# Where tile 1's first half statistics stand on VectorE: behind tile 0's first normalised half instead of ahead of tile 0's reciprocal

## The chip, the cores and the metric

The kernel runs on one core of one Trainium2 chip. The metric is the device time of one execution in microseconds (us), lower is better. A profile shows one execution. The experiments ran on four different chips, so kernels are compared by ratios within the same rounds. The "span" of a profile or run is the core's own time from first to last instruction; it is about 1.7 us less than the time.

## The reference, cut to what matters

```python
xn = _layernorm(x, axis=-1)                      # x: 2048 rows of 512, bf16
return x + _A_ref(xn, ...) + _B_ref(xn, ...)     # A: a state-space scan, B: a gated FFN

def _layernorm(x, axis=-1, eps=1e-5):
    m = jnp.mean(x, axis=axis, keepdims=True)
    v = jnp.var(x, axis=axis, keepdims=True)
    return (x - m) / jnp.sqrt(v + eps)
```

Every matmul of A and B reads `xn`, so nothing useful can run on TensorE before the first rows are normalised and transposed. The rows come in 16 tiles of 128. The first four tiles are the head of the kernel, and the change lies there.

## The kernel before: the parts that count

The program is a list of tasks with dependencies. A static scheduler puts them into one instruction list per engine; `order=` pins a task behind another. The loads of the head, and who issues them (SP's queue unless `eng="act"`):

```python
x_load(0)
x_load(1)
act_q = [dma("ld_touch", ..., eng="act")]
act_q.append(wg_load("a0", 0, 2, eng="act", ...))   # gate weights, 448 KB
x_load(2)                                           # each x tile: 128 KB
act_q.append(wg_load("a1", 2, 3, eng="act", ...))   # 224 KB
wg_load("a2", 3, 4)                                 # 224 KB
x_load(3)
# ... cut: further weights, x tiles 4 to 7
```

VectorE's pinned order for the four tiles of the head:

```python
last = ln_stat0(0, (bn_full(0),))        # tile 0: statistics, aggregate; ScalarE then takes the square root
last = bn_half(1, 0, order=(last,))      # tile 1: statistics of its first 256 columns
for a in range(4):
    last = g.add("dve", lambda e, a=a: e.reciprocal(out=rstd[:, a:a + 1], in_=sd0[:, a:a + 1]), ..., order=(last,))
    last = ln_half(a, 0, order=(last,))  # normalise columns 0 to 255 of tile a
    if a < 3:
        last = bn_half(a + 1, 1, order=(last,))
        last = ln_stat0(a + 1, (last,))
    last = ln_half(a, 1, order=(last,))
    if a < 2:
        last = bn_half(a + 2, 0, order=(last,))
```

Tile 0 uses statistics of all its 512 columns at once, the others of two halves. Each normalised half goes through two PE transposes into one PSUM bank, and ScalarE (for tile 3 VectorE) copies it to `xnT`. PE's order in the head is fixed: transposes of tile 0 (two pairs, with a few warming matmuls between, whose results nobody uses), 14 gate matmuls on tile 0's first half, the **third pair of transposes** (tile 1, first half), 14 gate matmuls on tile 0's second half, and so on; then the first 512-wide matmuls.

## Time and profile before

| | before |
|---|---|
| time, median of the runs in hand at the prediction | 180.02 us (179.74 to 180.13) |
| profiled execution | 180.3 us, span 178.6 us |
| PE busy / VectorE busy | 97% / 91% of the span |
| PE's share of the chain that ended last | 95% |

The page's first part, engine by engine (PE is TensorE, PEld its weight loads, DVE VectorE, ACT ScalarE, POOL GpSimd; SP, further down, is SyncE, which issues most loads; L509 means line 509 of the kernel):

```profile
span 178.6 us, 2421 instructions
PE 173.3 (97%) x929; PEld 83.9 (47%) x937; DVE 162.3 (91%) x281; ACT 88.7 (50%) x114; POOL 9.9 (6%) x21
```

The chain of waits that ended last, in order of time (start, duration, what):

```profile
1.25 3.50 DMA x_sb<-in_A_x_dram
...
4.78 0.43 DVE st L509
...
6.63 0.27 PE pb L565 x2
6.91 0.78 PE pb L780 x14
7.69 0.11 PE pb L565 x2
...
14.14 11.22 PE pb L739 x52
```

From 6.63 us on the chain is PE, piece against piece, to the end. What can be won is won ahead of that. There, the chain goes through a load of x (`x_sb`), then the half statistics at 4.78. The VectorE timeline of before shows what they held up (start, duration, instruction; in brackets the idle time before it and what ended it):

```profile
4.78 0.43 DVE L509 BATCH_NORM_STATS2 st<-x_sb 128x6 f32<-128x256 bf16 x1 [0.77 <-DMA x_sb<-in_A_x_dram]
5.12 0.15 DVE L531 RECIPROCAL rstd<-sd 128x1 f32<-128x1 f32 x1
5.31 0.35 DVE L514 TENSOR_SCALAR xn_sb<-x_sb,mv,rstd 128x256 bf16<-128x256 bf16 x1
...
6.36 0.42 DVE L509 BATCH_NORM_STATS2 st<-x_sb 128x6 f32<-128x256 bf16 x1
6.71 0.16 DVE L531 RECIPROCAL rstd<-sd 128x1 f32<-128x1 f32 x1
```

L509 at 4.78 is tile 1's half statistics, waiting 0.77 us for tile 1's data. Tile 0's reciprocal (L531) stands behind it, though its operand, ScalarE's square root, was ready at 4.33. L509 at 6.36 is tile 2's, in front of tile 1's reciprocal. And the PE timeline, with the first two pairs of transposes, the first gate group, and the third pair at 7.53:

```profile
5.80 0.27 PE L565 MATMUL pb<-ident,xn_sb 128*128 128x128 bf16 x2 [1.41 <-DVE xn_sb L514]
...
6.63 0.27 PE L565 MATMUL pb<-ident,xn_sb 128*128 128x128 bf16 x2 [0.23 <-ACT xnT L577]
6.75 0.94 PE L780 MATMUL pb<-xnT,wg 128*128 128x128 bf16 x14
7.53 0.28 PE L565 MATMUL pb<-ident,xn_sb 128*128 128x128 bf16 x2
```

The trace also records when each load's semaphore is complete. I call that the landing. In this execution tile 0 landed at 3.07 us, tile 1 at 4.76, tile 2 at 6.32.

### The profile page before, as it was taken

How to read it: one execution, taken by the hardware profiler on the slowest of the kernel's cores; microseconds unless marked ns; L12 is line 12 of the kernel's file. 1: busy time of each engine (PE TensorE's matmuls, PEld its weight loads, DVE VectorE, ACT ScalarE, POOL GpSimd, SP SyncE). 2: the span in 40 equal slices, each digit the busy share in tenths (PEclk: the TensorE clock that was granted, in tenths of full speed). 3: DMA queues.
4: the chain of work that ended last, by engine and by line, in shares of the span. 5: the costliest groups of instructions: out<-in, count | busy, mean ns of one | idle time of the engine just before them, and what ended most of it. 6: DMA issues, size and time to landing. Idle time of an engine off the chain costs nothing.

```text
span 178.6 us, 2421 instructions
## 1 busy us (share of the span) xinstructions
PE 173.3 (97%) x929; PEld 83.9 (47%) x937; DVE 162.3 (91%) x281; ACT 88.7 (50%) x114; POOL 9.9 (6%) x21
## 2 busy tenths in 40 slices
PE   7699999999999999999999999999999999999994
PEld 3595444443444444444444444444444444444743
DVE  1858985798899999999999999999999999999983
ACT  4369998999799957016565651000965620000000
POOL 3013400002300000040000000000000000000000
DMA  5995562669360000002420000001100000000122
GB/s 167 367 332 113 128 118 51 141 170 355 103 121 0 0 0 0 0 13 79 95 54 0 0 0 4 0 0 63 55 0 4 0 0 0 0 0 4 59 88 88
DMA packets 22978, 12.37 MB, mean 69 GB/s; under 512 B 15192, under 2 KB 22968, under 8 KB 22968
## 3 DMA queue, kind: packets, MB, share of 16 engines
q1 hardware_dynamic: 22472, 11.54, 23.5%
q10 hardware_dynamic: 496, 0.69, 1.2%
q8 instruction: 7, 0.11, 0.3%
q14 instruction: 3, 0.02, 0.1%
HBM read 6.46 MB, written 2.10 MB: 48 GB/s over the span
## 4 chain that ended last, share of the span: by engine, by line
PE 95%; DMA 2%; DVE 1%; issue 1%; SPq 0%; ACT 0%
PE pb L739 35%; PE pb L937 21%; PE pb L854 15%; PE pb L950 15%; PE pb L780 4%; DMA x_sb<-in_A_x_dram 2%; PE pb L817 2%; PE pb L827 1%; PE pb L565 1%; DVE st L509 0%; SPq L400 0%; ACT xnT L577 0%; DVE xn_sb L514 0%; DVE x_sb L955 0%; PE pb L562 0%
## 5 line engine op out<-in xcount | busy, mean ns | idle before, releaser
L894 DVE TENSOR_TENSOR_SCAN rot<-sm,car,rot 128x512 bf16<-128x512 f32 x32 | 39.0, 1267 | 0.1
L937 PE MATMUL pb<-wd,hT 128*128 128x512 bf16 (+3 forms) x194 | 38.1, 355 | 0.2
L739 PE MATMUL pb<-xnT,wu 128*128 128x512 bf16 x160 | 37.3, 379 | 0.0
L739 PE MATMUL pb<-xnT,wg 128*128 128x512 bf16 x132 | 31.3, 379 | 0.0
L950 PE MATMUL pb<-W,hss 128*128 128x512 bf16 (+2 forms) x140 | 28.1, 355 | 0.2
L854 PE MATMUL pb<-xnT,BT 128*128 128x512 bf16 x128 | 28.1, 379 | 0.0
L937 PEld LDWEIGHTS pb<-wd,hT 128*128 128x128 bf16 (+1 forms) x198 | 18.5, 98 | 19.9
L739 PEld LDWEIGHTS pb<-xnT,wu 128*128 128x128 bf16 x160 | 15.6, 98 | 18.9 <-issue 0.2
L751 ACT ACTIVATE sg<-pb 128x1024 bf16<-128x1024 f32 x20 | 20.1, 1025 | 8.6 <-PE pb L739 7.5
L807 ACT ACTIVATE uf<-pb 128x1024 bf16<-128x1024 f32 x20 | 20.6, 1028 | 6.8 <-PE pb L739 5.9
L950 PEld LDWEIGHTS pb<-W,hss 128*128 128x128 bf16 x144 | 13.5, 98 | 14.3
L739 PEld LDWEIGHTS pb<-xnT,wg 128*128 128x128 bf16 x132 | 12.7, 98 | 15.7 <-issue 0.8
L854 PEld LDWEIGHTS pb<-xnT,BT 128*128 128x128 bf16 x128 | 12.5, 98 | 15.1
L861 ACT ACTIVATE u_sb<-pb 128x1024 bf16<-128x1024 f32 x16 | 16.4, 1026 | 4.5 <-PE pb L854 4.2
L809 DVE TENSOR_TENSOR hT<-sg,uf 128x1024 bf16<-128x1024 bf16 x20 | 13.5, 682 | 1.0 <-ACT uf L807 0.9
L885 DVE TENSOR_TENSOR rot<-u_sb,cosT 128x2048 bf16<-128x2048 bf16 x8 | 9.7, 1219 | 2.8 <-ACT cosT L700 2.8
L955 DVE TENSOR_TENSOR x_sb<-pb,x_sb 128x512 bf16<-128x512 f32 (+2 forms) x18 | 10.9, 624 | 1.5 <-PE pb L950 1.4
L836 ACT ACTIVATE sg<-pb 96x1024 bf16<-96x1024 f32 x2 | 2.0, 1019 | 17.3 <-PE pb L817 17.3
L503 ACT ACTIVATE xn_sb<-x_sb,nmr,rstd 128x512 bf16<-128x512 bf16 x8 | 5.9, 802 | 9.3 <-DVE nmr L500 9.3
L885 DVE TENSOR_TENSOR rot<-rot,cosT 128x2048 bf16<-128x2048 bf16 x8 | 9.7, 1218 | 0.1
L885 DVE TENSOR_TENSOR rot<-rot,sin 128x2048 bf16<-128x2048 bf16 x8 | 9.8, 1219 | 0.0
L885 DVE TENSOR_TENSOR rot<-u_sb,sin 128x2048 bf16<-128x2048 bf16 x8 | 9.7, 1217 | 0.0
(78 smaller groups left out, 142.5 us busy)
## 6 DMA issues: line engine op xcount, KB each, us to landing
out_dram<-x_sb SPq DMA_DIRECT2D x15, 128.0 KB, 1.7
x_sb<-in_A_x_dram SPq DMA_DIRECT2D x3, 512.0 KB, 7.5
wd<-in_B_w_down_dram SPq DMA_DIRECT2D x1, 1280.0 KB, 7.1
wu<-in_B_w_up_dram SPq DMA_DIRECT2D x1, 768.0 KB, 5.4
wu<-in_B_w_up_dram SPq DMA_DIRECT2D x1, 608.0 KB, 7.5
x_sb<-in_A_x_dram SPq DMA_DIRECT2D x4, 128.0 KB, 4.1
wg<-in_B_w_gate_dram SPq DMA_DIRECT2D x1, 480.0 KB, 6.4
wg<-in_B_w_gate_dram ACTq DMA_DIRECT2D x1, 448.0 KB, 4.5
```

The costliest lines, as they stand in the source:

```text
L739: inst = e.matmul(pbank[0:fs, bk, :].rearrange("p (j t) -> p j t", j=4), lhsT=w[:, kt, i * 128:i * 128 + fs], rhs=xnT[:, c % 2, :, kt, :], ...
L751: g.add("act", lambda e: e.activation(out=sg[rows, sl, 0:n, :].rearrange("p a t -> p (a t)"), in_=pair_f32(rows, bk, 512 * n), func=AF.Sil ...
L780: inst = e.matmul(pbank[:, bk, q * 128:(q + 1) * 128], lhsT=wg[:, kt, i * 128:(i + 1) * 128], rhs=xnT[:, 0, q, kt, :], start=(kt == 0), st ...
L807: g.add("act", lambda e: e.activation(out=uf[rows, ul, 0:n, :].rearrange("p a t -> p (a t)"), in_=pair_f32(rows, bk, 512 * n), func=AF.Ide ...
L809: g.add("dve", lambda e: e.tensor_tensor(out=hT[rows, hb, i0:i0 + n, :], in0=sg[rows, sl, 0:n, :], in1=uf[rows, ul, 0:n, :], op=ALU.mult), ...
L854: inst = e.matmul(pbank[:, bk, :].rearrange("p (j t) -> p j t", j=4), lhsT=BT[:, ri, kt, pt * 128:(pt + 1) * 128], rhs=xnT[:, c % 2, :, kt ...
L861: g.add("act", lambda e: e.activation(out=u_sb[:, us].rearrange("p r t -> p (r t)"), in_=pair_f32(slice(0, 128), b0), func=AF.Identity), r ...
L885: tt = lambda out, a, b, op, r, w, nm: g.add("dve", lambda e: e.tensor_tensor(out=out, in0=a, in1=b, op=op), reads=r, writes=w, name="%s_% ...
L894: g.add("dve", lambda e, A0=A0, A1=A1, k=k, ri=ri, pt=pt: e.tensor_tensor_scan(out=A1[:, k, ri, :], data0=rr[:, pt:pt + 1].to_broadcast([1 ...
L937: inst = e.matmul(pbank[:, bk, 0:nc_], lhsT=hT[0:fs, hb, i, lt * 128:(lt + 1) * 128], rhs=wd[0:fs, i, c0:c0 + nc_], start=(i == 0), stop=F ...
L950: inst = e.matmul(pbank[:, bk, 0:nc_], lhsT=hss[:, hb, pt, ri, lt * 128:(lt + 1) * 128], rhs=W12[:, ri, pt, c0:c0 + nc_], start=False, sto ...
L955: g.add("dve", lambda e, bk=bk, a=a, c0=c0, nc_=nc_: e.tensor_tensor(out=x_sb[:, a, c0:c0 + nc_], in0=pbank[:, bk, 0:nc_], in1=x_sb[:, a, ...
```

## The change

The intent: tile 0 should not wait for tile 1's data. Its reciprocal and first normalised half go ahead, and tile 1's first half statistics come behind them.

```diff
             last = ln_stat0(0, (bn_full(0),))
-            last = bn_half(1, 0, order=(last,))
             for a in range(4):
                 last = g.add("dve", ... e.reciprocal(...) ..., order=(last,))
                 last = ln_half(a, 0, order=(last,))
+                if a == 0:
+                    last = bn_half(1, 0, order=(last,))
+                    last = ln_half(0, 1, order=(last,))
                 if a < 3:
                     last = bn_half(a + 1, 1, order=(last,))
                     last = ln_stat0(a + 1, (last,))
-                last = ln_half(a, 1, order=(last,))
+                if a:
+                    last = ln_half(a, 1, order=(last,))
                 if a < 2:
                     last = bn_half(a + 2, 0, order=(last,))
```

No instruction is added or removed.

## The prediction

> **What bounds the kernel.** TensorE. The page gives it 97% of the 178.6 us span, and the chain of waits that ended last is 95% PE. From 6.63 us on, that chain has hardly anything but PE groups, one against the next. Only the head is something else: the load of x tile 1, VectorE, ScalarE. A change in the head is worth what it moves the start of the unbroken PE stretch, and no more.
>
> **What the change moves.** No instruction is added or removed; VectorE's order in the head changes. In the VectorE timeline, the statistics of tile 0 end at 4.01 us and ScalarE's square root of tile 0 at 4.33, but VectorE stands idle (0.77 us, released by the x DMA) until 4.78, because the half statistics of tile 1 are next and x tile 1 has landed only at 4.76. The Trainium skill ("DVE: scalar operands, raw-bit mode, write accounting and state across instructions") calls the DVE's queue "one in-order queue"; this trace agrees: the reciprocal, ready at 4.33, runs at 5.12. After the change:
> - reciprocal 4.37 (was 5.12), first half of tile 0 4.57 to 4.92 (was 5.31), its PE transpose 5.06 (was 5.80), second transpose about 5.89 (was 6.63, after ScalarE's eviction), first gate matmuls about 6.01 (was 6.75). Their weights landed at 5.70.
> - Tile 1: second half of tile 0 at 5.17, second half statistics 5.38, aggregate 5.83 (was 6.02), square root done about 6.35 (was 6.67).
>
> **Why most of the 0.74 us is not kept.** The half statistics of tile 2 stand ahead of tile 1's reciprocal, and x tile 2's DMA is complete only at 6.33 us in this trace (before: that instruction started at 6.36, with no visible wait). The change brings VectorE there at 5.96; it waits until about 6.35. Then tile 1's reciprocal comes at about 6.70 (was 6.71), its first half at 6.90 to 7.25 (was 6.91). The transpose of tile 1 can start at 7.39, against 7.53 before, where it waited only for PE itself. So PE starts earlier, gets a new hole of about 0.4 us (6.95 to 7.39), and its unbroken stretch moves by about 0.14 us. Had x tile 2 landed early, the gain would be about 0.45 us (square root 6.35, reciprocal 6.39, transpose 7.08), and no more.
>
> After that the PE is unbroken as before.  Downstream waits have slack for 0.1 to 0.5 us: B's transposed load is complete at 22.8, needed at 25.4; the C weights are ready at 73.6, needed at 75.7; the last scan products at 168.5, needed at 171.1 (VectorE timeline against PE timeline). VectorE's work after 14.2 us is tied to the x4 load, not moved.
>
> **Prediction:** 179.83 us, between 179.45 and 180.15 with 80%. Faster by over 2%: 0.3%; same: 99.4%; slower: 0.3%.
>
> **What would show it.** VectorE timeline: no wait before the first reciprocal, which starts near 4.4; the x DMA's wait is now split: nothing or almost nothing before tile 1's first statistics (about 4.83), and a wait of about 0.2 us (engine-idle) before tile 2's. PE: first transpose near 5.06; first gate group near 6.0; a new wait for tile 1's normalised half (about 0.4 us) before the third pair of transposes; first 512-wide matmul at about 13.84 instead of 13.98.
>
> **What would make it wrong.** x tile 2 landing 0.2 us or more earlier in timed runs (gain up to 0.45), or later (gain to zero); the gate weights' loads (complete at 5.70, 6.61 and 7.17) becoming the wait; a later reorder on VectorE or ScalarE that costs the PE a wait; noise (0.4 us wide in three runs).

## The result, and the profile after

| | before | after |
|---|---|---|
| median of 4 timed runs | 179.96 us (179.74 to 180.13) | 179.99 us (179.85 to 180.09) |
| profiled execution: span | 178.6 us | 178.1 us |

The ratio of after to before is 1.0002, 95% interval 0.9984 to 1.0019. Ratios here are the mean time of one kernel's fast runs over that of the other's of the same rounds, so not quite the ratio of the medians quoted. So the time is the same, inside the predicted range. Yet the two profiles differ by 0.5 us in favour of after. The VectorE timeline of after:

```profile
4.34 0.16 DVE L530 RECIPROCAL rstd<-sd 128x1 f32<-128x1 f32 x1 [0.36 <-ACT sd L521]
4.54 0.35 DVE L514 TENSOR_SCALAR xn_sb<-x_sb,mv,rstd 128x256 bf16<-128x256 bf16 x1
4.80 0.42 DVE L509 BATCH_NORM_STATS2 st<-x_sb 128x6 f32<-128x256 bf16 x1
...
5.83 0.21 DVE L519 BATCH_NORM_AGGREGATE mv<-st 128x2 f32<-128x12 f32 x1
5.96 0.37 DVE L509 BATCH_NORM_STATS2 st<-x_sb 128x6 f32<-128x256 bf16 x1
6.41 0.16 DVE L530 RECIPROCAL rstd<-sd 128x1 f32<-128x1 f32 x1
```

The reciprocal of tile 0 now runs at 4.34, released by ScalarE, and tile 1's statistics at 4.80, with no wait. But tile 2's statistics at 5.96 did not wait either: in this execution tile 1 landed at 4.11 us and tile 2 at 5.40, far earlier than in the profile of before. No VectorE instruction can have done that; these loads wait for no engine, and were issued at 1.25 and 1.71 us in both profiles. The PE timeline and one line of the chain of after:

```profile
6.01 0.94 PE L783 MATMUL pb<-xnT,wg 128*128 128x128 bf16 x14
7.01 0.28 PE L568 MATMUL pb<-ident,xn_sb 128*128 128x128 bf16 x2
```

```profile
13.68 11.22 PE pb L742 x52
```

The third pair is at 7.01 instead of 7.53, and the 0.46 us by which the chain's 512-wide matmuls begin earlier (13.68 against 14.14) is kept to the end of the span. Two profiles therefore seem to show a gain of about half a microsecond which four timed runs do not show.

### The profile page after: what moved, and what is told of

It reads as the page before. It is cut to its first block, busy times and chain, and to the rows that moved or that the text cites. A ratio compares the mean times of both kernels' runs of the same rounds, so it can differ in the third digit from the quotient of the medians.

```text
span 178.1 us, 2421 instructions
## 1 busy us (share of the span) xinstructions
PE 174.4 (98%) x929; PEld 84.1 (47%) x937; DVE 162.3 (91%) x281; ACT 88.8 (50%) x114; POOL 10.3 (6%) x21
## 4 chain that ended last, share of the span: by engine, by line
PE 95%; DVE 2%; DMA 1%; issue 0%; ACT 0%
PE pb L742 36%; PE pb L940 21%; PE pb L857 16%; PE pb L953 15%; PE pb L783 3%; PE pb L820 2%; DMA x_sb<-in_A_x_dram 1%; PE pb L830 1%; PE pb L568 1%; DVE xn_sb L514 1%; DVE st L527 0%; DVE st L509 0%; ACT sd L521 0%; DVE mv L519 0%; DVE rstd L530 0%
## 5 line engine op out<-in xcount | busy, mean ns | idle before, releaser
L857 PE MATMUL pb<-xnT,BT 128*128 128x512 bf16 x128 | 28.1, 379 | 0.0
L857 PEld LDWEIGHTS pb<-xnT,BT 128*128 128x128 bf16 x128 | 12.5, 98 | 15.1
L503 ACT ACTIVATE xn_sb<-x_sb,nmr,rstd 128x512 bf16<-128x512 bf16 x8 | 5.9, 803 | 9.6 <-DVE nmr L500 9.6
```

What stands on the lines that cost most here:

```text
L503: g.add("act", lambda e, a=a: e.activation(out=xn_sb[:, a % NXN, :], in_=x_sb[:, a, :], func=AF.Identity, scale=rstd[:, a:a + 1], bias=nmr ...
L857: inst = e.matmul(pbank[:, bk, :].rearrange("p (j t) -> p j t", j=4), lhsT=BT[:, ri, kt, pt * 128:(pt + 1) * 128], rhs=xnT[:, c % 2, :, kt ...
```

## The experiments

Theory: **the two orders are decided by landings, which differ from one execution to the next.** If tile 1 lands late, the order of after is ahead; if it lands early, tile 1's half statistics fit under tile 0's square root in the order of before, and the order of after has put them into the path to tile 1's reciprocal for nothing. Rival: the head is really half a microsecond shorter, and it is **given back later**. Twelve kernels were run; all were correct. Ratios are to the kernel before in the same rounds.

| run | tile 1's load | tile 2's load | median us | ratio, 95% interval |
|---|---|---|---|---|
| e1_before_again | as is | as is | 179.79 | 1.0005 (0.9987 to 1.0022) |
| e1_after_again | as is | as is | 179.93 | 1.0008 (0.9994 to 1.0021) |
| e2_before_x1_late | third | second | 182.26 | 1.0136 (1.0112 to 1.0159) |
| e2_after_x1_late | third | second | 180.57 | 1.0051 (1.0034 to 1.0068) |
| e3_before_x_early | alone | behind weights | 182.31 | 1.0146 (1.0120 to 1.0172) |
| e3_after_x_early | alone | behind weights | 179.98 | 1.0025 (1.0004 to 1.0045) |
| e4_before_x1_late_warm | third | second | 181.50 | 1.0099 (1.0082 to 1.0116) |
| e5_before_x_first | alone | alone | 180.18 | 1.0007 (0.9994 to 1.0020) |
| e5_after_x_first | alone | alone | 180.43 | 1.0045 (1.0013 to 1.0076) |
| e6_before_x2_late | as is | last | 181.53 | 1.0077 (1.0057 to 1.0096) |
| e6_after_x2_late | as is | last | 181.06 | 1.0059 (1.0045 to 1.0074) |
| e7_before_x_first_x8_early | alone | alone | 179.83 | 1.0007 (0.9991 to 1.0023) |

### Both kernels once more, unchanged

No edit: these are second samples of the two heads.

> The kernel before, unchanged, as a second sample of its head. Landing theory (the sign and size of the change hang on when x tile 1 lands, and that differs between executions): time within 0.15 us of the kernel before; in its trace tile 1's x lands earlier than the 4.76 us of the first trace of before, about 4.1 to 4.5 us, and the third pair of transposes on PE starts at that landing plus 2.76 us (never before 6.76). Rival (the trace of before is typical and what the change gains at the head is given back later): x tile 1 lands at about 4.76 us again and that transpose starts at about 7.5 us.

> The kernel after, unchanged. Landing theory: ratio to before between 0.9990 and 1.0010; in its trace the third pair of transposes starts at 7.0 us if x tile 1 lands before 4.8 and x tile 2 before 6.0, at x tile 2's landing plus 1.0 us otherwise. Rival: the third pair starts about 0.45 us earlier than in the second trace of before, and a wait on PE that the kernel before does not have appears somewhere after 20 us.

The second profile of before has the span of after, 178.1 us. Its VectorE timeline:

```profile
4.34 0.43 DVE L509 BATCH_NORM_STATS2 st<-x_sb 128x6 f32<-128x256 bf16 x1 [0.36 <-DMA x_sb<-in_A_x_dram]
4.68 0.15 DVE L531 RECIPROCAL rstd<-sd 128x1 f32<-128x1 f32 x1
```

Tile 1 landed at 4.32 us here, not at 4.76, and the third pair of transposes ran at 7.09, which is that landing plus 2.77, as in the first profile (4.76 and 7.53):

```profile
7.09 0.28 PE L565 MATMUL pb<-ident,xn_sb 128*128 128x128 bf16 x2
```

The second profile of after shows tile 2 at 6.16 us and the wait that the prediction had spoken of, a short one:

```profile
5.88 0.21 DVE L519 BATCH_NORM_AGGREGATE mv<-st 128x2 f32<-128x12 f32 x1
6.18 0.43 DVE L509 BATCH_NORM_STATS2 st<-x_sb 128x6 f32<-128x256 bf16 x1
6.52 0.15 DVE L530 RECIPROCAL rstd<-sd 128x1 f32<-128x1 f32 x1
```

In the profile of after the statistics came 0.13 us behind the aggregate's start, here 0.30 us. The third pair came at 7.11, no earlier than in this second profile of before:

```profile
7.11 0.29 PE L568 MATMUL pb<-ident,xn_sb 128*128 128x128 bf16 x2 [0.21 <-DVE xn_sb L514]
```

PE is unbroken from there on in both. So the half microsecond between the first two profiles was mostly the landing of the loads: in this second pair the rival has no gain left that would have to be given back. (That an earlier head can be given back in other executions is shown further down, by e5.)

### Tile 1 made late

```diff
         x_load(0)
-        x_load(1)
+        x_load(2)
         act_q = [dma("ld_touch", ..., eng="act")]
         act_q.append(wg_load("a0", 0, 2, eng="act", ...))
-        x_load(2)
+        x_load(1)
```

> Kernel before with the loads of x tiles 1 and 2 swapped in their queue, so that tile 1 lands about 1.2 us later (5.4 to 6.3 us). Landing theory: the whole head follows tile 1's landing; third pair of transposes at landing plus 2.76 us, so 8.2 to 9.1 us; slower than before by 0.9 to 1.6 us. Rival (given back later): slower by less than 0.3 us, because a late head is absorbed downstream as the early one would be.

> Kernel after with the same swap. Landing theory: tile 0 goes ahead without tile 1 (first transpose at 5.05 us), third pair of transposes at tile 1's landing plus 2.23 us, so 7.6 to 8.6 us; faster than the swapped kernel before by 0.4 to 0.6 us. Rival (given back later): same as the swapped kernel before within 0.1 us.

The order of after is now 1.7 us faster (180.57 against 182.26). In the profile of after, tile 1 landed at 5.40 and the third pair came at 7.64, landing plus 2.24, as expected. In that of before, tile 1 landed at 5.86, but the third pair came at 9.34, not at 5.86 + 2.77 = 8.63. The time was 2.5 us over before, where at most 1.6 had been expected, and the distance between the two kernels three times the expected one: a second cost had been left out. The PE timeline of e2_before_x1_late shows it:

```profile
6.90 0.27 PE L565 MATMUL pb<-ident,xn_sb 128*128 128x128 bf16 x2 [2.09 <-DVE xn_sb L514]
...
7.85 1.70 PE L780 MATMUL pb<-xnT,wg 128*128 128x128 bf16 x14
...
9.55 1.70 PE L780 MATMUL pb<-xnT,wg 128*128 128x128 bf16 x14
...
11.26 0.95 PE L780 MATMUL pb<-xnT,wg 128*128 128x128 bf16 x14
```

Two groups of 14 took 1.70 us, the next one 0.95, and the granted clock (the share of TensorE's full rate, from the trace's clock records) was 1.00 from 6.0 to 7.8 us, 0.51 from 7.8 to 11.3, and 1.00 again after that. In the chain the same groups stand with 1.49 and 0.78 us, so 106 and 56 ns for each matmul. The Trainium skill ("TensorE: Matmul & The Clock Gate", section "Wait — 56ns, not 53.3ns?") gives 106.7 ns cold and 55.6 ns warm between starts of 128-column matmuls, and this trace agrees. PE had been idle for 2.09 us, waiting for tile 0, and then paid 0.71 us twice.

To test that, the swapped kernel before got 9 more warming matmuls ahead of the head (the scheduler's estimate was held, so the other engines' lists stayed the same):

```diff
-            pe_warm(9, 512, wbank)
+            pe_warm(18, 512, wbank)
```

> The kernel before with tile 1 landing late (loads of tiles 1 and 2 swapped), with 9 more warming matmuls at the start, so that PE has work until about 6.3 us. The swapped kernel before took 182.26 us, 1 us more than landing plus 2.76 us explains, and its trace shows the first two gate groups at 1.49 us instead of 0.78 each. Cold-array theory: with the extra warming both groups take about 0.78 us, and the time falls to about 180.8 us (180.5 to 181.3). Rival (the slow groups come of something else, as late gate weights): the groups stay at about 1.5 us and the time stays within 0.4 us of 182.26.

The groups took 0.78 us each again, as their first line in the PE timeline shows too:

```profile
8.33 0.94 PE L780 MATMUL pb<-xnT,wg 128*128 128x128 bf16 x14
```

The time fell by 0.76 us, to 181.50 (by the ratios, since the two ran in different rounds, by about 0.7). The fall is smaller than expected. In the profiled execution of this run tile 1 landed at 6.34, and the third pair came at 9.11, again landing plus 2.77. So the cold array accounts for part of what the late kernel lost, and the landing for at least part of the rest; the split in the timed runs isn't known, since only one execution of each has a profile. The granted clocks help a little: of the six runs of e2_before_x1_late, two (182.94, which is the profiled one, and 182.43) have 0.991, which is what 3.4 us at half rate make of 181 us, and the fastest (181.37) has 0.999. The other three read 1.0, which is also what an execution without clock records gets.

### Tile 1 made early

```diff
-        act_q.append(wg_load("a0", 0, 2, eng="act", ...))
+        wg_load("a0", 0, 2)
         x_load(2)
-        act_q.append(wg_load("a1", 2, 3, eng="act", ...))
+        wg_load("a1", 2, 3)
```

> Kernel before with the gate weights' loads moved from ScalarE's queue into the x loads' own queue, behind x tile 1, so that tile 1 lands without competition (about 3.5 us) and tile 2 at about 5.5. Landing theory: tile 1's half statistics fit under tile 0's square root, the reciprocal starts at about 4.36, the third pair of transposes at about 6.76 us (7.09 in the second trace of before): 0.2 to 0.4 us faster than before, and the faster one of this pair. Rival (the order before is worse in itself because its statistics stand ahead of the reciprocal): first transpose still at or after 5.36, not faster than the kernel after of this pair.

> Kernel after with the same move of loads. Landing theory: nothing to gain, the third pair of transposes stays at about 7.0 us (now set by tile 1's half statistics standing behind tile 0's first half), so slower than the kernel before of this pair by about 0.25 us (0.1 to 0.35), and within 0.1 us of the kernel after with its old loads. Rival: as fast as or faster than its partner.

The heads did what was expected of them. Tile 1 landed at 3.35 and 3.37 us. The third pair was at 6.95 in the order of before (tile 2, at 5.99, held it) and at 7.09 in that of after. But the time of before was 182.31, a clear miss. This edit changes the scheduler's estimates of the loads, and it put VectorE's and ScalarE's later instructions into another order. The chain of e3_before_x_early leaves PE at 51.17 us and is mostly VectorE after that. The pair tells about heads, not about totals.

So the experiment was made again. Now the loads are moved after scheduling, so that every compute engine's list stays exactly as it was, and tiles 0, 1 and 2 all go ahead of the gate weights:

```diff
         streams = _schedule(g.tasks, engs)
+        wga = [t for t in streams["act"] if t.name in ("ld_wga0", "ld_wga1")]
+        x2 = [t for t in streams["sp"] if t.name == "ld_x2"]
+        streams["act"] = [t for t in streams["act"] if t not in wga]
+        for t in wga:
+            t.eng = "sp"
+        rest = [t for t in streams["sp"][2:] if t not in x2]
+        streams["sp"] = streams["sp"][:2] + x2 + wga + rest
```

> Kernel before with x tiles 0, 1, 2 first and then the gate weights, all in one queue, and with every compute engine's order held as it is in before (the scheduler's reordering of the last attempt is shut out). Landing theory: tile 1 at about 3.4 us and tile 2 at about 3.8, half statistics of tile 1 under the square root, reciprocal at about 4.40, third pair of transposes at 6.8 to 6.9 us, first 512-wide matmul at 13.25 to 13.4; 0.15 to 0.4 us faster than before and with a narrower spread than before's. Rival (the order before is worse in itself): no faster than its partner with the order after.

> Kernel after with the same loads. Landing theory: tile 1's half statistics still stand behind tile 0's first half at about 4.85, third pair of transposes at about 7.05 to 7.1 us, so slower than its partner by 0.2 to 0.3 us, and within 0.15 us of after with its old loads. Rival: as fast as its partner or faster.

Tile 1 landed at 3.37 and 3.42 us. The third pair was at 6.84 in the order of before and at 7.13 in the order of after; the first 512-wide matmul at 13.29 and 13.64. The third pair in e5_before_x_first, then in e5_after_x_first:

```profile
6.84 0.28 PE L565 MATMUL pb<-ident,xn_sb 128*128 128x128 bf16 x2
```

```profile
7.13 0.28 PE L568 MATMUL pb<-ident,xn_sb 128*128 128x128 bf16 x2
```

With early data **the order of before is the faster head**, by 0.3 us. The medians go the same way (180.18 against 180.43), though five of the six runs of after lie anywhere from 180.2 to 181.8 and the intervals are wide. Against the kernel before, however, nothing was won: 180.18 against 180.03 in the same rounds, where 0.15 to 0.4 us less had been expected. The chain of e5_before_x_first says where an earlier head goes:

```profile
41.20 6.83 PE pb L739 x32
48.03 1.41 ACT xn_sb L503 x2
49.44 0.92 ACT uf L807
50.36 0.05 issue
50.41 8.81 PE pb L739 x40
```

PE waits for an eviction (L807), which stands on ScalarE behind the normalisation of tiles 8 to 11 (L503). That hangs on the load of these tiles, which landed at 40.82 us, behind a row of transposed loads that wait for one another. The order of after had the same wait, to 50.42. So there is a second limit, which an earlier head runs into. How near it is in the unchanged kernel is read from the VectorE timeline. In this run the last small VectorE step before L503 (L500) came at 46.24 us, in the first profile of before, without a visible wait of PE, at 46.19:

```profile
40.80 2.47 DVE L479 BATCH_NORM_STATS2 st<-x_sb 128x6 f32<-128x512 bf16 x4 [0.82 <-DMA x_sb<-in_A_x_dram]
...
46.19 0.16 DVE L500 SCALAR_TENSOR_TENSOR nmr<-mv,rstd 128x4 f32<-128x4 f32 x1 [0.86 <-POOL rstd L491]
```

In both, PE reaches the next group, L854, at the same time, 59.21 us with the wait and 59.26 without it. In the execution of the first profile of before, then, a head earlier by more than about 0.1 us could not have shortened the span (an estimate from these four numbers). By the same reckoning the first profile of after (L500 at 45.67, its L857 at 58.80) had 0.16 us left. In the two e1 profiles L500 came at 44.82 and 44.89 us, and there was room. By this estimate the rival holds in part for some executions of the unchanged kernels too; no run tests it there.

### Tile 2 made late

```diff
         act_q.append(wg_load("a0", 0, 2, eng="act", ...))
-        x_load(2)
         act_q.append(wg_load("a1", 2, 3, eng="act", ...))
         wg_load("a2", 3, 4)
         x_load(3)
+        x_load(2)
```

> Kernel before with x tile 2 loaded last of the four (about 7.3 us instead of 5.4 to 6.3), tile 1 as it was. The step of the prediction that the half statistics of tile 2 in front of tile 1's reciprocal pass tile 2's landing on to tile 1: reciprocal of tile 1 at tile 2's landing plus 0.37 us, third pair of transposes at that landing plus 1.0 to 1.1 us (about 8.3 us), time about 1.2 us over before; if PE then runs its first groups at half rate (1.5 us instead of 0.78), up to 1 us more. Rival: tile 2's landing delays tile 2's own transposes only; third pair below 7.6 us.

> Kernel after with tile 2 loaded last. If that step holds, the order of tile 1's statistics no longer matters: third pair of transposes at tile 2's landing plus 1.0 to 1.1 us as in its partner (about 8.3 us), and the times of the two agree within 0.3 us, although the first transposes come at 5.0 us here and between 5.2 and 5.8 there. Rival: after keeps a lead or a lag of its own of more than 0.4 us.

This tests the prediction's claim that tile 2's statistics, standing in front of tile 1's reciprocal, pass tile 2's landing on. VectorE in e6_before_x2_late, then in e6_after_x2_late:

```profile
7.02 0.43 DVE L509 BATCH_NORM_STATS2 st<-x_sb 128x6 f32<-128x256 bf16 x1 [1.22 <-DMA x_sb<-in_A_x_dram]
7.36 0.14 DVE L531 RECIPROCAL rstd<-sd 128x1 f32<-128x1 f32 x1
```

```profile
7.46 0.43 DVE L509 BATCH_NORM_STATS2 st<-x_sb 128x6 f32<-128x256 bf16 x1 [1.30 <-DMA x_sb<-in_A_x_dram]
7.80 0.15 DVE L530 RECIPROCAL rstd<-sd 128x1 f32<-128x1 f32 x1
```

Tile 1's reciprocal comes in both 0.34 us behind the start of tile 2's statistics. Tile 2 landed at 6.99 and 7.44, and the third pair came at 7.95 and 8.39, landing plus 0.96 and 0.95. So the mechanism holds, in both orders alike. The times, 181.53 and 181.06, lie 0.47 us apart where 0.3 had been allowed, and over the 0.4 us that had been named as a lead of after's own: a miss. The profiled heads lie 0.44 us apart the other way round, and that difference is the landings'. The profiled run of before was the fastest of its four (180.78), that of after the slowest of its four (181.25), so the landings of the other six may well differ, but that isn't shown.

### Both limits taken away

```diff
+        by = {t.name: t for t in streams["sp"]}
+        x8, cre, cim, xtd = by["ld_x8"], by["ld_cre"], by["ld_cim"], by["xTd1"]
+        x8.deps = (x8.deps - {cim}) | {xtd}
+        cre.deps = cre.deps | {x8}
+        streams["sp"].remove(x8)
+        streams["sp"].insert(streams["sp"].index(cre), x8)
```

> The x-first kernel before of the last job, with one thing more: the load of x tiles 8 to 11 is issued ahead of the two transposed loads of C instead of behind them; every compute engine's order is unchanged. In the x-first kernels PE waited from about 48.0 to 50.4 us for an eviction that stands behind ScalarE's normalisation of tiles 8 to 11, whose data landed at 40.82 and 40.85 us. Second-limit theory (an earlier head is given back there): those tiles land before 34 us, that wait is gone, PE is unbroken from the head (first 512-wide matmul at 13.2 to 13.4) to the end, span 177.7 to 177.9, time 179.4 to 179.65 in nearly every run, 0.5 us below the x-first kernel before and 0.2 to 0.5 us below before. Rival (the wait at 48 us has another cause, as ScalarE's or VectorE's own load): the wait stays and the time stays at 180.0 to 180.3.

In the profile it is as expected: tiles 8 to 11 landed at 32.35 us, the wait at 48 us is gone, the third pair is at 6.82, and the chain is PE from the head to the end, with a span of 177.9 us:

```profile
41.19 17.37 PE pb L739 x80
58.56 6.91 PE pb L854 x32
```

So the second limit was what stopped the profiled execution of e5. But that execution was the slowest of its five timed runs (180.26), and the one profiled here is the fastest of its six (179.59). The timed runs are spread from 179.59 to 180.26, only two of six in the expected band, and the ratio to before is 1.0007, the same as e5's. The version that was meant to beat both kernels doesn't. What holds its slower executions is open: only the fast one has a profile. Gate weights or later loads, which this order puts further back, are possible, and nothing here shows it.

## Why the prediction was right, and where it was not

All profiles together give a plain rule for the third pair of transposes. The unit is us; the load that rules is in bold.

| profile | tile 0 | tile 1 | tile 2 | third pair | ruling landing + |
|---|---|---|---|---|---|
| before | 3.07 | **4.76** | 6.32 | 7.53 | 2.77 |
| e1 before | 3.04 | **4.32** | 5.42 | 7.09 | 2.77 |
| e4 before | 3.11 | **6.34** | 4.63 | 9.11 | 2.77 |
| e5 before | **3.13** | 3.37 | 4.28 | 6.84 | 3.71 |
| e7 before | **3.11** | 3.36 | 4.00 | 6.82 | 3.71 |
| e3 before | 3.11 | 3.35 | **5.99** | 6.95 | 0.96 |
| e6 before | 3.17 | 4.02 | **6.99** | 7.95 | 0.96 |
| after | **3.04** | 4.11 | 5.40 | 7.01 | 3.97 |
| e5 after | **3.17** | 3.42 | 4.17 | 7.13 | 3.96 |
| e3 after | **3.12** | 3.37 | 5.72 | 7.09 | 3.97 |
| e2 after | 3.13 | **5.40** | 4.04 | 7.64 | 2.24 |
| e1 after | 3.09 | 4.21 | **6.16** | 7.11 | 0.95 |
| e6 after | 3.16 | 4.23 | **7.44** | 8.39 | 0.95 |

(e2 before, with its cold array, is left out: 5.86 + 2.77 + 0.71 = 9.34.) Before is held by the latest of tile 0 + 3.71, tile 1 + 2.77, tile 2 + 0.96; after by the latest of tile 0 + 3.97, tile 1 + 2.24, tile 2 + 0.95. The change buys 0.53 us on tile 1's path and sells 0.26 us on tile 0's. The constants are fitted to these same profiles, and the 2.24 rests on one of them. With tile 2 out of the way the change breaks even where tile 1 lands 3.97 - 2.77 = 1.20 us behind tile 0. With the unchanged loads that distance was 1.69, 1.28, 1.07 and 1.12 us in the four profiles of the two kernels: on both sides of the break-even point.

The rule also tells (an estimate) what the other order would have made of the same landings. With those of the first profile of before, after would have had its third pair at 7.27, 0.26 us ahead; with those of the first profile of after, before would have had it at 6.88, 0.13 ahead of the measured 7.01; with those of the two e1 profiles, after is 0.08 ahead and level. With after's landings, then, the order gave none of the 0.52 us between the first two profiles. Over these four sets of landings after is ahead by about 0.05 us at the third pair. It loses as much behind it: from there to the first 512-wide matmul PE took 6.45 us in both profiles of before and 6.51 in both of after; why isn't shown.

Point by point:

- **What bounds the kernel** was right: PE is unbroken behind the head in all four profiles of the unchanged pair.
- **The reciprocal at 4.37, tile 0's first half at 4.57, the first gate group at 6.01**: measured 4.34, 4.54 and 6.01. "No wait before the first reciprocal" was badly put: a wait of 0.36 us is there, for ScalarE's square root; the one for the load is gone.
- **"Why most of the 0.74 us is not kept"** was right in its mechanism and shown by e6. It was not what happened in the profile of after, where tile 2 had landed at 5.40 and the statistics started at once; in e1_after_again tile 2's statistics started 0.17 us later behind the aggregate (0.30 us against 0.13), and tile 1's reciprocal 0.06 us later (0.64 us behind it against 0.58), since that reciprocal waits for ScalarE's square root as well. The new wait of PE before the third pair, predicted at about 0.4 us, is not visible in the profile of after and is 0.21 us in e1_after_again.
- **"Had x tile 2 landed early, the gain would be about 0.45 us"** is the step that failed, by its premise and not by its sum. With tile 1 at 4.76 the rule gives 0.49 us (7.53 against 7.04). But it keeps tile 1 at 4.76 while tile 2 is early, because one trace of before was taken for the kernel; the list of what would make the prediction wrong has tile 2's landing and not tile 1's. When both land early, before has no wait to lose, and after is behind: 0.3 us in e5.
- **The size**: 0.19 us less was predicted from the two medians 179.83 and 180.02; measured were +0.03 us in the medians of the result, and the ratio 1.0008 in e1. The landings of the first trace of before (its execution took 180.3 us, above every timed run then in hand) made the gain look larger than it is in the other three profiles' landings. That the range held says little: it contains 180.02, the time of no change at all. The predicted sign was not confirmed, so the hit is in part luck.
- **Nothing given back downstream** was right for the four profiles of the unchanged pair, but with less room than the prediction listed: it had checked the weights of B and C and the scan, not the load of tiles 8 to 11.

In the timed runs after has the narrower spread: 179.83 to 179.98 in the six of e1, against 179.50 to 180.44 for before in the eleven of the same rounds. That fits the rule, because after's head depends less on tile 1. It is argued, not shown, since of each kernel's executions in those rounds at most one has a trace.

The landings themselves hang on what else is being loaded. With the gate weights issued from ScalarE's queue, the load issued second landed between 4.02 and 4.76 us; with them behind it in one queue (e3, e5, e7), between 3.35 and 3.42. This agrees with the Trainium skill ("DMA: Bandwidth & Descriptors", section "Issuing engines are not separate DMA queues"): loads from different engines run on the same DMA engines and interleave.

## What to carry to other kernels

An instruction that waits for a load, put ahead of a ready one on an in-order engine, is free only as long as the load comes inside a gap that is there anyway; moving it behind costs time whenever the load is early (here 0.26 us, for an instruction of 0.42 us). Before trusting a gain of a few tenths of a microsecond in two traces, take a second trace of the unchanged kernel and compare when the loads landed in each. And when an experiment reorders loads under a static scheduler, hold the other engines' lists fixed, or the scheduler's new order will be measured instead (e3).

## What the Trainium skill lacked or had wrong

- "DMA: Bandwidth & Descriptors" gives no figure for how much the landing of one load differs between executions of one program. Tile 1's load, unchanged in program and place, landed at 4.76, 4.11, 4.32 and 4.21 us in four executions, a range of 0.65 us, more than the whole effect of the change.
- No page has the cost of the batch-norm statistics on VectorE. Here 128x512 bf16 took 0.69 us, 128x256 took 0.37 to 0.43 us, and the aggregate of 6 or 12 values a row 0.18 to 0.21 us. An independent VectorE instruction behind the 256-column statistics started 0.34 us after their start, the aggregate that needs them 0.45 us.
- "TensorE: Matmul & The Clock Gate", section "What's actually happening", gives an idle window of about 3.4 us for the fall to the slow clock. In e2_before_x1_late PE stood idle for 2.09 us at one stretch, ran two pairs of transposes and three warming matmuls around a wait of 0.23 us, and was at a granted clock of 0.51 from 7.8 to 11.3 us. The page doesn't say how much work inside a window still counts as idle. e6_after_x2_late, with its third pair at 8.39 us behind a gate group that began at 6.02 us and takes 0.94, stayed at full rate, with a wait of 1.43 us before that pair.
